# Seven half-size products in place of eight in the last batch's first channel product, with an order written out as a table and DMA issues on two queues

## The chip, the cores and the metric

The kernel runs on one core of a Trainium2 chip. The metric is the device time of one execution in microseconds (us), as the median of several runs. The core has five engines that run beside each other: TensorE (PE) multiplies matrices, VectorE (DVE), ScalarE (ACT) and GpSimd (POOL) work element by element, and SyncE (SP) issues DMAs. Each takes its instructions in the order of its own queue and waits on semaphores for the others.

## The reference

Four batches, 768 tokens, 8 heads of 64: window attention with four sink tokens, then one MLP block of a token product and two channel products.

```python
scores = where(keep, q @ k.T / sqrt(64), -1e9)      # keep: sink or within 128 tokens back
x = softmax(scores) @ v                             # (4, 768, 512)
tok = einsum('ts,bsd->btd', w_tok, alpha1 * x + beta1)
u = x + lam * tok
a2 = alpha2 * u + beta2
ch = maximum(a2 @ w_ch1, 0.0) @ w_ch2               # 512 -> 2048 -> 512
out = u + lam * ch
```

## The kernel before

Every piece of work is a *task*: a Python function that issues a few instructions, with a priority, the engines that may do it and the ns that each is thought to take, the tasks it comes after, and the buffers it uses. `plan.add` collects the tasks. At the end `plan.emit` sets the order. A planner (`Plan.run`) imitates the engines: it takes the task that can start soonest, breaks ties by priority, gives it an engine and a free buffer of its kind, and imitates the DMA rings as well (`Rings`). Priorities are shuffled a little by a list of thirty random seeds (`TURNS`) ahead of that. Where the planner sees TensorE idle in the first 36 us it adds short filler matmuls ("idle", L349) that keep its clock up.

Buffers come in kinds with a fixed number of places (`homes`). The ones that matter here: `d`, four PSUM banks for products; `S`, two pairs of PSUM banks for attention scores; `wst`, four buffers of SBUF for staged weights and, in batches 2 and 3, for the fp16 q and k of one head pair; `n16`, four; `nat`, eight, for loaded q and k, and later for sums; `vnat`, four, for loaded v; `x`, twelve rows of 128 tokens by 512; `uT` and `qkT`, one each; `hT`, two.

The stages of a batch, for the names in the profile:

- attention (`scores` L724, `pv` L825, and the normalising multiply L851): of batch b+1, spread among the products of batch b. In batches 2 and 3 q and k are loaded (L508), cast to fp16 and turned by a DMA transpose (L630); earlier by TensorE (`tp`).
- token product (`tok` L956): six row tiles of six matmuls. Then x gets the sum (L963), is cast (L356) into `u16`, transposed by DMA into `uT` (L1015) and scaled in place by alpha2 and beta2 (`affine`, L980 on ACT, L982 on DVE). Batch 0 transposes on TensorE (`uTp`).
- first channel product (`mlp1`, L1036): for each of two halves of the tokens (`chk`, 384 tokens) and each of 16 tiles of 128 hidden channels (`fi`) four matmuls that add over the 512 inputs into one `d` bank; then a relu into `hT` by ACT (L1042) or DVE (L1044).
- second channel product. Batch 0: `mlp2` (L1221). Batches 1 to 3: the 2 x 2 block product (token halves by channel halves) in Winograd's form with seven products P1 to P7 (`prod`, L1153) in place of eight. Its sums of weights (`w2_sums`, L1068) are made once, its sums of h (`h_sums`, L1094 to L1097, called S1 to S4) for every batch.

The weights of the first channel product are in `w1f` (128 x 4 x 2048, fp16), where the second index is the quarter of the 512 inputs. All DMAs but the casting loads (GpSimd) and five tiny ones at the start (ACT) are issued by SyncE.

Of the kernel before, what the change touches and what calls it, by code (L numbers as in the profile page):

```python
# [9 lines left out]
FP32 = mybir.dt.float32  # L10
# [7 lines left out]
SEEN = {PE: 200, ACT: 60, DVE: 60, POOL: 70}  # L18


class Buf:


    def __init__(self, kind, shape, dtype, name):
        self.kind, self.shape, self.dtype, self.name = kind, shape, dtype, name
        self.left = 0
        self.freed = 0.0
        self.home = None
        self.t = None


FW = 1.0

SWDONE = 1800.0


class Rings:


    WIRE = {"hw": 1600.0, "sw": 2100.0}  # L40

    HOLDS = 128.0

    def __init__(self):
        self.now = 0.0
        self.queue = {"hw": [], "sw": []}
        self.given = {"hw": [], "sw": []}

    def issue(self, ring, t, at):
        self.given[ring].append(t)  # L50
        self.queue[ring].append([t, float(t.lands[0]), float(t.lands[1]), at + self.WIRE[ring]])

    def room(self, ring, lands, at):

        keep = self.now, {r: [list(h) for h in q] for r, q in self.queue.items()}
        self.step(at)
        g = self.given[ring]
        last = g[-8] if len(g) >= 8 and g[-8].seen is None else None
        q = self.queue[ring]
        while last is not None and any(h[0] is last for h in q):  # L60
            self.step(float("inf"))
        over = sum(h[1] for h in q) + lands[0] - self.HOLDS
        while ring == "hw" and over > 0 and q:
            if q[0][1] < over:
                self.step(float("inf"))
                over = sum(h[1] for h in q) + lands[0] - self.HOLDS
            else:
                self.now += over * q[0][2]
                over = 0
        to = max(at, self.now)  # L70
        self.now, self.queue = keep
        return to

    def step(self, until):

        while True:
            heads = [(r, q[0]) for r, q in self.queue.items() if q]
            if not heads:
                return None
            live = [(r, h) for r, h in heads if h[3] <= self.now]  # L80
            later = [h[3] for r, h in heads if h[3] > self.now]
            turn = sum(h[2] for r, h in live)
            ends = [(self.now + h[1] * turn, r) for r, h in live]
            end = min(ends) if ends else (float("inf"), None)
            to = min([end[0], until] + later)
            for r, h in live:
                h[1] -= (to - self.now) / turn
            self.now = to
            if end[0] <= to:
                return self.queue[end[1]].pop(0)[0]  # L90
            if to >= until:
                return None

    def peek(self):

        keep = self.now, {r: [list(h) for h in q] for r, q in self.queue.items()}
        t = self.step(float("inf"))
        at = self.now if t else float("inf")
        self.now, self.queue = keep
        return at  # L100
# [11 lines left out]
class Plan:  # L112
# [19 lines left out]
    def run(self, prio):  # L132

        tasks = self.tasks
        rank = [0] * len(tasks)
        for r, i in enumerate(sorted(range(len(tasks)), key=lambda i: (prio[i], i))):
            rank[i] = r
        waiting = [len(t.needs) for t in tasks]
        ready = [t.since for t in tasks]
        homes = {k: [0.0] * n for k, n in self.homes.items()}  # L140
        busy = {k: [False] * n for k, n in self.homes.items()}
        for t in tasks:
            t.seen = None
            for b in t.uses:
                b.left, b.freed, b.home = 0, 0.0, None
        for t in tasks:
            for b in t.uses:
                b.left += 1
        free = {PE: 0.0, ACT: 3500.0, DVE: 3200.0, POOL: 500.0, SP: 0.0}
        rings = Rings()  # L150
        open_ = []
        steps = []

        def end(t, seen):
            t.seen = seen
            for b in t.uses:
                b.left -= 1
                b.freed = max(b.freed, seen)
                if b.left == 0:
                    busy[b.kind][b.home] = False  # L160
                    homes[b.kind][b.home] = b.freed
            for o in t.then:
                ready[o.i] = max(ready[o.i], seen)
                waiting[o.i] -= 1
                if not waiting[o.i]:
                    bisect.insort(open_, (rank[o.i], o.i))

        def pick():
            best = None
            spare = {k: sorted(h for h, x in zip(homes[k], busy[k]) if not x) for k in homes}  # L170
            for r, i in open_:
                at = ready[i]
                if best is not None and at > best[0]:
                    continue
                t = tasks[i]
                asked = {}
                for b in t.uses:
                    if b.home is None:
                        asked[b.kind] = asked.get(b.kind, 0) + 1
                if any(len(spare[k]) < n for k, n in asked.items()):  # L180
                    continue
                at = max([at] + [spare[k][n - 1] for k, n in asked.items()])
                own = None
                for e in t.engs:
                    at_e = max(free[e], at)
                    if e == POOL or (e == DVE and t.port):
                        at_e = max(at_e, port)
                    key = (at_e + FW * t.engs[e], at_e, r, at_e + t.engs[e], i, e)
                    if own is None or key < own:
                        own = key  # L190
                if best is None or own[1:] < best:
                    best = own[1:]
            return best

        open_ = sorted((rank[t.i], t.i) for t in tasks if not waiting[t.i])
        mode = None
        port = 0.0
        landing = float("inf")
        until, _, took = self.fill
        while len(steps) < len(tasks):  # L200
            best = pick()
            if best is None or landing <= best[0]:
                assert landing < float("inf"), "no task can go on"
                t = rings.step(float("inf"))
                end(t, rings.now + (SWDONE if POOL in t.engs else 300.0))
                landing = rings.peek()
                continue
            start, r, _, i, e = best
            open_.pop(bisect.bisect_left(open_, (r, i)))
            t = tasks[i]  # L210
            for b in t.uses:
                if b.home is None:
                    b.home = min((h, n) for n, (h, x) in enumerate(zip(homes[b.kind], busy[b.kind]))
                                 if not x)[1]
                    busy[b.kind][b.home] = True
            idle = None
            n = int((start - max(free[PE], 400.0)) / (took if free[PE] > 4500.0 else 110.0))
            if e == PE and free[PE] < until and n > 0:
                spare = [(h, k) for k, (h, x) in enumerate(zip(homes["d"], busy["d"])) if not x]
                if spare and min(spare)[0] <= free[PE]:  # L220
                    idle = (min(spare)[1], n)
                    homes["d"][idle[0]] = start
                    mode = None
            cost = t.engs[e]
            if t.lands:
                cost += rings.room("sw" if e == POOL else "hw", t.lands, start) - start
            if e == PE:
                if start < 4500.0:
                    cost = cost * 2
                if t.mode != mode:  # L230
                    cost = cost + 95
                mode = t.mode
            free[e] = start + cost
            if e == POOL or (e == DVE and t.port):
                port = free[e]
            steps.append((t, e, start, free[e], idle))
            if t.lands:
                rings.step(start)
                rings.issue("sw" if e == POOL else "hw", t, free[e])
                landing = rings.peek()  # L240
            else:
                end(t, free[e] + SEEN[e])
# [1187 lines left out]
```

The softmax here doesn't subtract the row's maximum and nothing guards it: scores larger than these inputs give would overflow.

## Time and profile before

| what | value |
|---|---|
| median of 3 runs | 256.87 us (256.66 to 257.07) |
| the profiled execution | 257.06 us, of it a span of 255.3 us from the first instruction to the last |
| granted TensorE clock | 0.999 |
| last token product of batch 3 ends | 212.84 us |
| first channel product of batch 3 | 212.84 to 233.63 us |
| second channel product of batch 3 | 233.63 to 252.01 us, then one add and the last store |
| one first-product matmul (L1036) | 128 x 384, 512 of them in all batches |
| relu of a product on ACT (L1042) | 0.49 us |
| relu of a product on DVE (L1044) | 0.55 us |
| add of a 256-column product on DVE (L1166) | 0.42 us |
| DMA transpose, from issue to landing | 2.4 us (`uT`), 2.8 us (`qkT`) |

The busy time of an engine is the time in which it works on an instruction; the chain of waits follows the end of the program back, at each step to what released it. Matmuls overlap, and their ends are modelled, so a long row of matmuls in the chain is TensorE without a gap.

### The profile page before, as it was taken

Reading aid. Unit: us, or ns where it says so; the run is one execution under the profiler, and the core shown is the slowest. Engines: PE = TensorE matmul, PEld = TensorE weight load, DVE = VectorE, ACT = ScalarE, POOL = GpSimd, SP = SyncE. Lnnn points to the kernel's source line nnn. Section 1 sums busy time; section 2 is a strip of 40 time slices with the busy share of each in tenths; the row PEclk is TensorE's granted clock in tenths of the full one; section 3 lists DMA queues with packets and bytes.
Section 4 is the critical chain, followed back from the end, with each engine's and each line's share of the span. In section 5 each row is a group of like instructions: output and inputs, shape, how many; then the busy total and the mean of one; then the engine's idle time right before and its main releaser. Section 6 shows DMA issues by size and latency. Waiting matters only on the chain.

```text
span 255.3 us, 5519 instructions
## 1 busy us (share of the span) xinstructions
PE 247.4 (97%) x2174; PEld 160.9 (63%) x2174; DVE 190.0 (74%) x402; ACT 142.6 (56%) x236; POOL 88.3 (35%) x108
## 2 busy tenths in 40 slices
PE   8999998999999999899999999999999999999994
PEld 7754645675555544456678676558668666667883
DVE  6777998696878878578889997877789764136782
ACT  2689845989848035688971225867571125775000
POOL 7409802344445330159653460735310101000000
PEclk9999999999999999999999999999999999999999
DMA  6998999999943998599778689501000156000105
GB/s 202 195 223 292 216 230 392 373 370 218 218 73 115 186 260 190 117 205 220 155 138 182 125 191 251 85 3 21 3 0 3 59 167 146 0 0 3 63 4 185
DMA packets 86130, 38.80 MB, mean 152 GB/s; under 512 B 73540, under 2 KB 80460, under 8 KB 86104
## 3 DMA queue, kind: packets, MB, share of 16 engines
q1 hardware_dynamic: 82320, 35.14, 56.5%
q0 software_dynamic: 3744, 3.28, 8.1%
q8 instruction: 17, 0.28, 0.5%
q14 instruction: 9, 0.07, 0.1%
q10 hardware_dynamic: 40, 0.03, 0.0%
HBM read 29.91 MB, written 6.29 MB: 142 GB/s over the span
## 4 chain that ended last, share of the span: by engine, by line
PE 88%; DMA 4%; DVE 3%; POOL 1%; issue 1%; ACT 1%; POOLq 0%; ACTq 0%
PE h L1036 33%; PE P L1153 21%; PE tok L956 11%; PE ch L1221 8%; PE pv L825 5%; PE S L724 4%; DMA n<-in_q_dram 4%; DVE uT L982 1%; PE S L719 1%; PE tp L614 1%; PE pv L818 1%; POOL n L497 1%; PE wT L916 1%; ACT uT L980 1%; DVE w2f L1068 1%
## 5 line engine op out<-in xcount | busy, mean ns | idle before, releaser
L1036 PE MATMUL h<-uT,w1f 128*128 128x384 f16 x512 | 91.9, 326 | 2.7 <-DVE uT L982 1.3
L1036 PEld LDWEIGHTS <-w1f 128*128 128x128 f16 x512 | 47.3, 98 | 34.5 <-issue 5.5
L1042 ACT ACTIVATE hT<-h 128x384 f16<-128x384 f32 x99 | 48.3, 492 | 26.1 <-PE h L1036 25.6
L1153 PEld LDWEIGHTS <-hT 128*128 128x128 f16 x408 | 39.8, 98 | 6.7
L746 ACT ACTIVATE E<-S 128x1024 f16<-128x1024 f32 (+1 forms) x39 | 37.9, 1001 | 7.5 <-PE S L724 3.7
L869 POOL TENSOR_TENSOR tm<-x,la_b 128x512 f32<-128x512 f32 x18 | 26.2, 1454 | 26.3 <-DVE xh L872 19.1
L956 PE MATMUL tok<-xh,wtokT 128*128 128x512 f16 x144 | 33.4, 379 | 0.0
L356 ACT CAST u<-x 128x512 f16<-128x512 f32 x19 | 11.7, 618 | 31.2 <-DVE x L963 31.1
L1153 PE MATMUL P<-w2f,hT 128*128 128x256 f16 x216 | 25.9, 273 | 0.0
L1166 DVE TENSOR_TENSOR x<-x,P 128x256 f32<-128x256 f32 x45 | 18.3, 418 | 8.2 <-PE P L1153 7.9
L1044 DVE TENSOR_SCALAR hT<-h 128x384 f16<-128x384 f32 x29 | 15.8, 553 | 10.9 <-PE h L1036 10.5
L956 PEld LDWEIGHTS <-wtokT 128*128 128x128 f16 x144 | 14.0, 98 | 14.6
L1221 PE MATMUL ch<-w2f,hT 128*128 128x512 f16 x96 | 23.0, 379 | 0.0
L1153 PE MATMUL P<-w2s,hT 128*128 128x256 f16 x192 | 22.8, 273 | 0.0
L851 DVE TENSOR_TENSOR x<-pv,rec 128x256 f32<-128x256 f32 x48 | 20.4, 424 | 1.7
L358 POOL CAST vfs<-vnat 128x512 f16<-128x512 f32 x18 | 15.0, 840 | 16.2 <-DMA vnat<-in_v_dram 16.0
L963 DVE TENSOR_TENSOR x<-x,tok 128x512 f32<-128x512 f32 x24 | 16.2, 684 | 5.7 <-PE tok L956 5.7
L356 ACT CAST n<-nat 128x768 f16<-128x768 f32 x16 | 13.2, 829 | 10.8 <-DMA nat<-in_q_dram 8.8
L825 PEld LDWEIGHTS <-E 128*128 128x128 f16 x328 | 15.2, 97 | 6.0 <-issue 1.6
L825 PE MATMUL pv<-vfs,E 128*128 128x65 f16 x328 | 17.9, 194 | 0.0
L358 POOL CAST u<-x 128x512 f16<-128x512 f32 x5 | 3.1, 621 | 34.8 <-DVE x L963 21.1
L1221 PEld LDWEIGHTS <-hT 128*128 128x128 f16 x96 | 8.6, 98 | 9.1 <-issue 0.2
(131 smaller groups left out, 327.4 us busy)
## 6 DMA issues: line engine op xcount, KB each, us to landing
out_dram<-x SPq DMA_DIRECT2D x21, 256.0 KB, 2.8
nat<-in_q_dram SPq DMA_DIRECT2D x13, 384.0 KB, 5.3
nat<-in_k_dram SPq DMA_DIRECT2D x13, 384.0 KB, 5.7
vnat<-in_v_dram SPq DMA_DIRECT2D x18, 256.0 KB, 5.2
wst_w<-in_moe_w_ch_dram SPq DMA_DIRECT2D x8, 512.0 KB, 7.4
wtn<-in_moe_w_tok_dram SPq DMA_DIRECT2D x6, 384.0 KB, 4.7
w1f<-in_moe_w_ch_dram POOLq DMA_DIRECT2D x4, 512.0 KB, 11.1
v<-in_v_dram SPq DMA_DIRECT2D x12, 128.0 KB, 6.4
```

The source lines that it names most:

```text
L356: nc.scalar.copy(o, i)
L358: engine[e].tensor_copy(o, i)
L746: nc.scalar.activation(eT.t, pS.t[:, :, 0 : n * w].rearrange("p e (i w) -> p e i w", i=n), AF.Exp, scale=scale)
L825: nc.tensor.matmul(po.t[:, hl, :], eT.t[:, e_, off + i, c : c + P], vf[j][:, h, :], start=(r < 2 and n == 0), stop=(n == len(parts) - 1 an ...
L851: nc.vector.tensor_mul(bx.t[:, 4 * G : 4 * G + 4, :], po.t[:, :, 0:D], rec.t.to_broadcast([P, 4, D]))
L869: engine[e].tensor_mul(bt.t, bx.t.rearrange("p h d -> p (h d)"), la1_b)
L956: nc.tensor.matmul(pt.t, wtokT[:, si, ti * P : (ti + 1) * P], hs[si].t, start=(si == 0), stop=(si == NR - 1))
L1036: nc.tensor.matmul(ph.t, w1f[:, c, fi * P : (fi + 1) * P], bu.t[:, c, chk * NTOK : (chk + 1) * NTOK], start=(c == 0), stop=(c == NC - 1))
L1042: nc.scalar.activation(bh.t[:, fi, :], ph.t, AF.Relu)
L1153: nc.tensor.matmul(pc.t, hh[:, nt * P : (nt + 1) * P], w(fi), start=(first and n_ == 0), stop=(n_ == HF - 1), skip_group_check=True)
L1166: nc.vector.tensor_add(row(bx)[:, cols], row(bx)[:, cols], pc.t)
L1221: nc.tensor.matmul(pc.t, bh.t[:, fi, nt * P : (nt + 1) * P], w2f[:, fi, :], start=(fi == 0), stop=(fi == NF - 1))
```

## The change

Three things change together.

**The first channel product of batch 3.** It takes Winograd's form too. The blocks are: token halves c0 and c1 of `uT`, input halves (quarters 0-1 and 2-3), and hidden tiles i and i + 8. For each pair of tiles (i, i + 8), i = 0 to 7, seven products P1 to P7 of two matmuls stand where four tiles of four matmuls stood. `NPL = 0` says that no pair keeps the plain form.

```diff
+    HSUM = 3
+    NPL = 0
+    def w1_sums(p):
+        n = (HF - NPL) * P
+        for w in ("S1", "S2", "S4"):
+            w1s[w] = Buf("wst", [P, 2, n], FP16, f"w1{w}")
...
+            sub(0, "S1", lambda g, c: g.tensor_add(b1.t[:, c], w1f[:, c, k_], w1f[:, 2 + c, k_]), [done["w1", 3]], [b1])
+            sub(1, "S2", lambda g, c: g.tensor_sub(b2.t[:, c], b1.t[:, c], w1f[:, c, f]), [done["w1S1", c]], [b1, b2])
+            sub(2, "S4", lambda g, c: g.tensor_sub(b4.t[:, c], w1f[:, 2 + c, f], b2.t[:, c]), [done["w1S2", c]], [b2, b4])
+            sub(3, "S3", lambda g, c: g.tensor_sub(w1f[:, c, k_], w1f[:, c, f], w1f[:, c, k_]),
+                [done["w1S1", c]] + late, [])
...
+    def u_sums(p, b):
+        for w in ("T1", "T2", "T3", "T4"):
+            uS[w] = Buf("n16", [P, 2, NTOK], FP16, f"u{w}")
...
+        sub(0, "T3", lambda g: g.tensor_sub(t3.t, bu.t[:, 2:4, c1], bu.t[:, 0:2, c1]), ud(0, 0) + ud(1, 0) + ud(1, 1), [t3])
+        sub(0.1, "T1", lambda g: g.tensor_sub(t1.t, bu.t[:, 0:2, c1], bu.t[:, 0:2, c0]), ud(0, 0) + ud(1, 0), [t1])
+        sub(0.2, "T2", lambda g: g.tensor_sub(t2.t, bu.t[:, 2:4, c1], t1.t), [done["uT1"]] + ud(1, 1), [t1, t2])
+        sub(0.3, "T4", lambda g: g.tensor_sub(t4.t, bu.t[:, 2:4, c0], t2.t), [done["uT2"]] + ud(0, 1), [t2, t4])
```

`mlp1_pair` takes one `S` buffer (two banks, V and Q), one `d` bank X for P2, two fp32 buffers of kind `vnat` and one of kind `x`. P1 goes to V and is read out; P6 adds to V and is read out; P5 adds to V and is read out; P3 adds to V, and its relu is one tile of h. P2 goes to X, and adding P1's copy gives the second tile. P7 goes to Q; the sum with P5's copy gives the third. P4 adds to Q; with P6's copy it gives the fourth. These three sums are an add on DVE (fp32 copy + PSUM, into `hT`) and a relu in place on ACT, DVE or POOL.

```diff
+        def mm(e):
+            for c in range(2):
+                nc.tensor.matmul(acc(), lhs(c), rhs(c), start=first and c == 0, stop=c == 1, skip_group_check=True)
+        before = {"P6": "P1", "P5": "P6", "P3": "P5", "P4": "P7"}.get(what)
+        if before:
+            after = after + [done["hread", before, i]]
...
+        def plus(bx, chk, fi, more, acc=acc):
+            bh = hT[b, chk]
+            r = add(p + 0.05, {DVE: 485}, lambda e: nc.vector.tensor_add(bh.t[:, fi, :], bx.t, acc()), [a] + more, [po, bx, bh])
...
+        if what == "P1":
+            done["hread", "P1", i] = read(ba)
+        elif what == "P2":
+            plus(ba, 0, i, [done["hread", "P1", i]])
+        elif what == "P6":
+            done["hread", "P6", i] = read(bb)
+        elif what == "P5":
+            done["hread", "P5", i] = r = read(bc)
+            done["hread", "P7", i] = plus(bc, 1, HF + i, [r, done["hp", "P7", i]], lambda: two.t[:, 1, 0:NTOK])
+        elif what == "P4":
+            plus(bb, 0, HF + i, [done["hread", "P6", i]])
```

**The order.** The planner, its ring model and the seeds go. In their place are four tables: `ORDER`, the numbers of all 1227 tasks in the order in which they are issued; `ENGINES`, a digit for each task; `HOMES`, a place for each buffer; `IDLES`, where filler matmuls stand. The costs at `plan.add` and the spacing of priorities (`PAR`) change too, but the tables alone set what is issued. The order differs from the one before in all batches.

```diff
-    def emit(self, turns):
-        prio = [t.prio for t in self.tasks]
-        for seed in turns:
-            prio = shuffle(prio, seed)
-        for t, e, start, stop, idle in self.run(prio):
+    def emit(self, order, engines, homes, idles):
+        own = iter(homes)
+        for t in self.tasks:
             for b in t.uses:
                 if b.home is None:
+                    b.home = int(next(own), 16)
+        fills = {i: (home, n) for i, home, n in idles}
+        for i in order:
+            t = self.tasks[i]
+            e = (ACT, DVE, PE, POOL, SP)[int(engines[i])]
+            idle = fills.get(i)
...
+    IDLES = (
+        (46, 0, 64), (53, 0, 2), (90, 1, 6), (107, 1, 13), (111, 1, 3), (150, 2, 1), (158, 0, 1),
+    )
```

**Two queues.** Plain loads and stores may be issued by SyncE or by ACT; transposes stay with SyncE.

```diff
+    queue = {SP: nc.sync, ACT: nc.scalar}
...
-                p, {SP: 480}, lambda e: nc.sync.dma_start(bf.t, src), [wait], [bf], lands=(16, {(0, 0, 1): 85, (0, 1, 0): 140}.get((b, hp, t), 72)))
+                p, {SP: 480, ACT: 550}, lambda e: queue[e].dma_start(bf.t, src), [wait], [bf], lands=(16, {(0, 0, 1): 85, (0, 1, 0): 140}.get((b, hp, t), 68)))
```

By the tables 27 issues are ACT's: one load of w_tok, ten of q and k, six of v, and ten stores, two in batch 0 and eight in the later ones.

## The prediction

> **What bounds the kernel now.** I read the page's shares first, then the chain of waits, then what TensorE waited for, then groups and windows of the last batch.
>
> ```profile
> PE 247.4 (97%) x2174; PEld 160.9 (63%) x2174; DVE 190.0 (74%) x402; ACT 142.6 (56%) x236; POOL 88.3 (35%) x108
> ...
> DVE  6777998696878878578889997877789764136782
> ACT  2689845989848035688971225867571125775000
> ```
>
> TensorE fills 97% of the span, so only two things can shorten it: fewer matmuls, or fewer TensorE gaps. In the slices, DVE and ACT thin out in the last fifth, where no next batch's attention is left.
>
> The chain of waits (start us, us, what) ends in one unbroken run of matmuls:
>
> ```profile
> 211.54 1.29 PE tok L956 x6
> 212.84 20.80 PE h L1036 x128
> 233.63 18.35 PE P L1153 x168
> 252.01 0.42 DVE x L1166
> ```
>
> 20.80 us is the first channel product of the last batch: 128 matmuls of 384 columns, 162.5 ns each, no gap. The 18.35 us behind it (second product) and the last add and store are no part of the edit. TensorE's waits, longest in total (us, times, longest):
>
> ```profile
> PE h L1036 <- DVE uT L982: 1.3, 2, 1.1
> ...
> PE h L1036 <- ACT uT L980: 0.9, 2, 0.5
> ...
> PE h L1036 <- DVE x L1166: 0.4, 1, 0.4
> ```
>
> They lie at 39.8-41.4 us (start of batch 0's first product, 0.47 + 0.19 + 0.38), 101.8-103.4 (batch 1's, 1.07 and a little) and 180.2. The same stretches in the timeline:
>
> ```profile
> 39.78 0.32 PE L1036 MATMUL h<-uT,w1f 128*128 128x384 f16 x1 [0.47 <-ACT uT L980]
> ...
> 102.83 2.49 PE L1036 MATMUL h<-uT,w1f 128*128 128x384 f16 x12 [1.07 <-DVE uT L982]
> ```
>
> Windows of the last two stages, and of the time from 19 us to them, show what room the evacuating engines have:
>
> ```profile
> 212.70:233.50 20.80, 20.80 (x130) 12.52 (x129) 5.77 (x9) 15.18 (x31) 0.61 (x1) 1.00 0.11 27
> 233.50:252.05 18.55, 18.47 (x169) 16.31 (x167) 14.24 (x30) 0.88 (x3) 0.00 (x0) 1.00 0.20 72
> 19.00:212.70 193.70, 190.97 (x1643) 119.11 (x1640) 156.22 (x323) 115.65 (x186) 79.37 (x85) 1.00 0.72 169
> ```
>
> After the length: PE, PEld, DVE, ACT, POOL busy. In the first product DVE has 15.0 us free, ACT 5.6. From 19 to 212.7 us TensorE idles 2.7 us.
>
> **What the Trainium skill says.** "TensorE: Matmul & The Clock Gate", section "Wait — 56ns, not 53.3ns?": a warm matmul costs its columns over 2.4 GHz and about 2.5 ns; for 384 columns 162.5 ns, and the trace agrees to the digit (20.80 / 128). The same page, "Architectural detail": ACT and DVE are strict first-in-first-out, so an instruction that waits holds all behind it. "DMA: Bandwidth & Descriptors", section "Issuing engines are not separate DMA queues": issuing from several engines saves only the time of the issue; no run here shows it. "SBUF — State Buffer", section "Who interferes with whom": a DVE operation with two SBUF inputs contends with a GpSimd operation that reads SBUF; the trace of before has such adds (0.42 us for 512 fp16 columns, one of 0.55), too few to settle it.
>
> **The change, part by part.** The sum is made against the profiled execution: 257.06 us, of it a span of 255.3. The median shown is 256.87, 0.19 lower. The written-out order is numbers, but counting the tasks in the order in which the code adds them gives each number its name, and so each engine's order and each tile's buffer.
>
> *Products.* Each of 8 tile pairs has 7 products of 2 matmuls where it had 4 x 4: 112 for 128, all of 384 columns. 16 x 162.5 ns = 2.6 us less.
>
> *Waits inside the pairs.* A pair's bank is now read three times between products (P1, P6, P5, P3 share one bank, P7 and P4 the other). A product that needs a read can start after: 0.16 us drain and 0.04 to ACT (h ends 233.63 by the model, ACT starts 233.67), the read 0.49 (L1042), 0.04 back: 0.73 us from the last issue of the one to the first of the other. A product issues in 0.33. Two pairs run interleaved, so two other products (0.65) usually stand between: 0.08 short, about twice a round. Where the next two pairs take over the banks, the last relu and add (0.49 on ACT, 0.55 on DVE, between 0.42 for 256 and 0.68 for 512 columns) are in the way. Laying out the queues of all three engines in the new order with these durations, I get for the four rounds waits of 0.1, 0.3 + 0.15, 0.15 + 0.15 and 0.5, and 0.1 in the last round: 1.4 us in all. The ends: 0.6 if reads overlap better (ACT instructions back to back start closer than their duration), 4 if DVE lags. For DVE is nearly full: 23 adds at 0.48 (spacing when back to back), three sums of u at 0.47, three of h at 0.88 (of eight; four lay in this stage before), some nine relus, two reads and two adds of batch 2 come to 18.8 us in a stage of 19.8.
>
> *Entry.* All pairs need sums of both halves of u. After the last token product seven products of batch 2 and five of the pairs (7 x 0.873 + 5 x 0.33 = 7.75 us) are queued; the add (0.69), cast (0.62), transpose (2.4), affines and two sums come to about 7.5 us by DVE's queue, seven adds included. Hidden by 0.2 us; each further us late costs one.
>
> *Sums of w1.* Eight of 1024 fp16 columns, by the mask multiply of the same size (0.73) 5.8 us, seven on DVE and one on POOL in batches 0 to 2; the last two overwrite w1 beside batch 2's second product. They take three of the four staging buffers "wst" for good. Batch 3's q and k therefore go through one buffer, a head pair after the other. The last pair's load waits for batch 2's sum buffer (product P7 of batch 1); from there 0.5 us issue, 5.3 landing (median), two casts 1.6, two transposes 2.5 and 2.8 give 12.7 us, and 15.4 us of matmuls stand before its first score. Hidden, with 2.7 us to spare.
>
> *Moves.* Batch 0's h now starts behind a whole token product (1.29 us) that covers the affines: 0.9 of its 1.04 us goes. In batch 1 the first three token products come first, and 7.0 us of other matmuls follow before h, against about 6.6 us for add, cast, transposes and affines: 0.9 of 1.17 goes, and the next thing late would be the last affine on DVE, behind three adds. At 180 us h waited for a PSUM buffer that two adds had to read; the new order gives it another: 0.3 of 0.37. Together 2.1 (ends: 0 and 2.4).
>
> *Start.* q and k of the first heads are asked for before the 384 KB of w_tok that now lead SyncE's queue. The filler matmuls behind the first transpose are 26 for 43. But all loads share 16 engines that are 90% busy from 6 us on, and POOL now has a multiply ahead of its last load (1.45 us in L869 for that size). I take 0.5 us of gain; ends 1.5 and a loss of 1.
>
> *Two queues.* 27 issues go to ACT's queue. In the trace ACT's own issues took 0.27 to 0.58 us: some 14 us of ACT, spread over 250, and each with a wait holds what is behind it. Some stand before exps and relus in batches 0 and 1. With the DVE sums above and small new gaps of any reorder I put this at 1.0 us lost; ends 0 (ACT idles 113 us) and 5.
>
> Sum: -2.6 + 1.4 - 2.1 - 0.5 + 1.0 = -2.8; 257.06 - 2.8 = 254.3, and on the scale of the median **254.1 us**.
>
> **The rivals.**
> *All of it.* Waits in pairs 0.6, gaps 2.4, start 1.0, nothing lost: -5.4, 251.5 us. For it: ACT and DVE are free in that stage. Against: TensorE's order is in-line, and four dependent reads a pair don't vanish.
> *DVE paces the pairs.* If an add costs its whole 0.55 and a relu its whole latency, DVE's 18.8 becomes 21.5, the stage is longer than the 20.8 of now, and the saved matmuls are given back: +0.7 for -1.2, total -0.9, 256.0 us. For it: 95% full with waits in line. Against: adds back to back start 0.33 us apart where one lasts 0.42.
> *ACT's queue holds TensorE* (the slower side). The stores and loads that SyncE now takes sat there waiting for as much as 26 us at no cost; on ACT an issue that waits for a buffer or a DVE add holds exps and relus, and scores and h stop when their two or four PSUM buffers are full. If one in three of the 27 holds TensorE for its 0.54 us, 4.9 us are lost in place of 1.0: 258.0; with half of the closed gaps lost to it too, 259.0. It decides from 3.8 us lost, 0.14 us an issue. Against: most are placed behind their waits.
> That the products are not saved isn't a rival: the loop has no plain h left for the last batch.
>
> **How the numbers follow.** Forecast 0.55, all of it 0.13, DVE paces 0.15, ACT's queue 0.17. About 0.2%, 0.5 us, is what a measurement can tell from no change. The forecast's own ends are 252 to 256.5; the first rival asks for 251.5 and below, part of the last for 258 and over. 8 in 10: 251.2 to 258.2. Faster: nearly all of the first two, half of the third: 0.68. Same 0.08, slower 0.24, the last rival and half of the reach of the third.
>
> **What would show it.** Right: 112 matmuls in the pairs with TensorE waits of 1 to 2 us among them, each for an ACT read or DVE add; no wait of over 0.3 us at the start of batches 0's and 1's h; the second product of batch 3 still about 18.4 us. Wrong: a DVE busy without a gap through the pairs while TensorE waits over 3 us; scores of batch 3 waiting for transposes; ACT issues just ahead of TensorE gaps in batches 0 to 2; first transposes later than now (7.5 us).

## The result and the profile after

| | before | after |
|---|---|---|
| median | 256.97 us (256.66 to 258.39, 4 runs) | 267.96 us (266.63 to 269.61, 4 runs) |
| the profiled execution | 257.06 us, span 255.3 | 266.63 us, span 264.9 |
| granted TensorE clock | 0.999 | 0.991 |

The ratio is 1.042, with a 95% interval of 1.034 to 1.050: slower. The page of the changed kernel, shares and slices:

```profile
PE 247.2 (93%) x2142; PEld 159.0 (60%) x2142; DVE 209.3 (79%) x449; ACT 138.5 (52%) x230; POOL 113.9 (43%) x130
...
DVE  6495899789989863898999895867589896778981
ACT  1559853888984141899532235766613446663000
```

TensorE is busy for as long as before (247.2 us for 247.4), though it has 32 matmuls less (16 of the products and 16 fillers); its idle time grew from 7.9 to 17.7 us. DVE took 19 us more, and the thin last fifth of its row has filled up. The two traces side by side say where the 9.6 us of span went. Batch 2's last products stand among the pairs now, and some of batch 3's second product; the table takes them out at 0.109 us for a matmul (32 of them ahead of the stage, which starts at 212.33 us, and 8 behind it, which ends at 241.48 us). The start of batch 0's product before is taken without its waits: 41.38 us less three matmuls that had run by then.

| up to | before | after | late by |
|---|---|---|---|
| batch 0's first product runs | 40.89 | 43.94 | 3.05 |
| start of batch 3's first product | 212.84 | 215.82 | 2.98 |
| end of batch 3's first product | 233.63 | 240.61 | 6.98 |
| the last add ends | 252.43 | 259.40 | 6.97 |
| the span ends | 255.3 | 264.9 | 9.6 |

Three places, then: 3.0 us ahead of batch 0's product, 4.0 us in the pairs, where the sum had 1.2 us less, and 2.6 us behind the last add. What TensorE waited for (us in all, times, longest; `hp` are the two banks V and Q of a pair):

```profile
PE hp L1028 <- DVE hT L1042: 2.5, 5, 0.5
PE h L935 <- DVE uT L881: 2.1, 1, 2.1
PE pv L724 <- ACT E L645: 1.9, 1, 1.9
PE tok L855 <- DVE x L862: 1.1, 1, 1.1
...
PE hp L1028 <- ACT hT L1069: 0.6, 2, 0.5
PE hp L1028 <- ACT hb L155: 0.4, 2, 0.2
```

**The start.** The timeline of ACT and of TensorE at 16 to 21 us:

```profile
16.14 0.61 ACT L645 ACTIVATE E<-S 128x512 f16<-128x512 f32 x1
19.70 0.35 ACTq L441 DMA_DIRECT2D wtn<-in_moe_w_tok_dram  x1
20.10 1.02 ACT L645 ACTIVATE E<-S 128x1024 f16<-128x1024 f32 x1 [3.35 <-DMA v<-in_v_dram]
...
21.18 0.43 PE L724 MATMUL pv<-vfs,E 128*128 128x65 f16 x7 [1.86 <-ACT E L645]
```

ACT does nothing from 16.75 to 19.70 us: the next thing in its queue is the issue of a load of w_tok, and what ends its idle time is the landing of a load of v, which has no buffer in common with it. The chain of waits names that load:

```profile
14.98 4.70 DMA v<-in_v_dram
19.70 0.35 ACTq L441
```

In the trace the issues of SyncE and ACT take eight completion semaphores in turn (numbers 107, 109, 111 and 113 to 117). The issue at 19.70 us takes number 109, which the load of v at 14.98 us had taken eight issues before, and so it waits for that load to land. The exp behind it is 3.35 us late, and TensorE waits 1.86 us for that exp. From 20 to 25 us the granted clock is 0.66. One more 1.05 us goes at 41.4 us: two adds of DVE (L780) take 2.81 us beside two products of GpSimd (L837, 2.94 us); the same add takes 0.65 us at 37.2. The Trainium skill, "SBUF — State Buffer", section "Who interferes with whom", says that a DVE operation with two SBUF inputs contends with a GpSimd operation that reads SBUF; these numbers agree.

**The pairs.** The chain of waits through the first round (start, us, what):

```profile
218.42 0.74 PE hp L1028 x4
219.16 0.02 issue
219.19 0.49 ACT hc L155
219.68 0.02 issue
219.70 0.56 DVE hT L1042
220.26 0.04 issue
220.31 0.82 PE hp L1028 x4
221.13 0.02 issue
221.16 0.50 ACT hT L1069
...
222.15 0.56 DVE hT L1042
222.71 0.02 issue
222.73 0.50 ACT hT L1069
```

TensorE, ACT and DVE take turns. At 219.19 ACT reads bank V into `hc` and is done at 219.67; then DVE's add at 219.70 reads bank **Q**; only behind that does TensorE go on at 220.31, with P3, which writes bank **V**. ACT had been done with V 0.6 us before. In the same way a relu of ACT, which reads V (L1069), stands behind adds of DVE that read Q, though both only read. A pair's V and Q are one buffer of two banks (`hp`), and the waits are made by buffer.

**The end.** The last stores in the timeline, and the last add:

```profile
256.27 4.62 SPq L1192 DMA_DIRECT2D out_dram<-x  x4
...
257.05 3.86 ACTq L1192 DMA_DIRECT2D out_dram<-x  x5
...
258.98 0.42 DVE L1186 TENSOR_TENSOR x<-x,P 128x256 f32<-128x256 f32 x1 [0.45 <-PE P L1173]
```

All nine stores of batch 3's second product are issued from 256.3 us on. Before, they began at 236.7. Three of them follow P2 and its add, and their data is complete more than 15 us before the end; in the order they stand near its end, two on ACT's queue and one on SyncE's, behind stores of later products. From the last add to the end it takes 5.5 us in this execution; before it took 2.9.

### The profile page after: what moved, and what is told of

Same layout as the page of the kernel before. It is cut to its first block, busy times and chain, and to the rows that moved or that the text cites. A ratio compares the mean times of both kernels' runs of the same rounds, so it can differ in the third digit from the quotient of the medians.

```text
span 264.9 us, 5543 instructions
## 1 busy us (share of the span) xinstructions
PE 247.2 (93%) x2142; PEld 159.0 (60%) x2142; DVE 209.3 (79%) x449; ACT 138.5 (52%) x230; POOL 113.9 (43%) x130
## 4 chain that ended last, share of the span: by engine, by line
PE 79%; DMA 5%; DVE 5%; SPq 4%; ACT 3%; issue 2%; ACTq 0%; DVEq 0%
PE h L935 24%; PE P L1173 21%; PE tok L855 8%; PE ch L1241 7%; PE pv L724 5%; PE hp L1028 5%; DMA v<-in_v_dram 4%; PE S L623 3%; DVE hT L1042 2%; SPq L441 1%; DVE x L780 1%; PE S L618 1%; PE pv L717 1%; SPq L430 1%; DMA uT<-u 1%
## 5 line engine op out<-in xcount | busy, mean ns | idle before, releaser
L935 PE MATMUL h<-uT,w1f 128*128 128x384 f16 x384 | 68.7, 326 | 2.1 <-DVE uT L881 2.1
L935 PEld LDWEIGHTS <-w1f 128*128 128x128 f16 x384 | 35.6, 98 | 24.8 <-issue 4.4
L1173 PEld LDWEIGHTS <-hT 128*128 128x128 f16 x408 | 39.8, 98 | 7.1 <-issue 0.2
L768 POOL TENSOR_TENSOR tm<-x,la_b 128x512 f32<-128x512 f32 x18 | 24.6, 1368 | 37.6 <-DVE rec L749 15.1
L943 DVE TENSOR_SCALAR hT<-h 128x384 f16<-128x384 f32 x47 | 25.4, 553 | 7.8 <-PE h L935 7.1
L941 ACT ACTIVATE hT<-h 128x384 f16<-128x384 f32 x49 | 23.3, 492 | 13.4 <-PE h L935 13.1
L155 ACT CAST n<-nat 128x768 f16<-128x768 f32 x21 | 17.1, 832 | 16.3 <-DMA qkT<-n 12.8
L724 PE MATMUL pv<-vfs,E 128*128 128x65 f16 x328 | 18.2, 196 | 1.9 <-ACT E L645 1.9
L585 POOL TENSOR_SCALAR_AFFINE_SELECT E<-E 128x512 f16<-128x512 f16 x20 | 13.1, 681 | 14.4 <-ACT E L645 14.3
L157 POOL CAST vfs<-vnat 128x512 f16<-128x512 f32 x18 | 12.2, 692 | 12.2 <-DMA vnat<-in_v_dram 5.9
L749 DVE RECIPROCAL rec<-pv 128x4 f32<-128x4 f32 x48 | 8.5, 177 | 8.7 <-PE pv L724 8.1
```

The source lines that it names most:

```text
L155: nc.scalar.copy(o, i)
L724: nc.tensor.matmul(po.t[:, hl, :], eT.t[:, e_, off + i, c : c + P], vf[j][:, h, :], start=(r < 2 and n == 0), stop=(n == len(parts) - 1 an ...
L768: engine[e].tensor_mul(bt.t, bx.t.rearrange("p h d -> p (h d)"), la1_b)
L935: nc.tensor.matmul(ph.t, w1f[:, c, fi * P : (fi + 1) * P], bu.t[:, c, chk * NTOK : (chk + 1) * NTOK], start=(c == 0), stop=(c == NC - 1))
L941: nc.scalar.activation(bh.t[:, fi, :], ph.t, AF.Relu)
L943: nc.vector.tensor_scalar_max(bh.t[:, fi, :], ph.t, 0.0)
```

## The experiments

Each kernel below has 4 to 22 runs. They come in four sets: all issues on SyncE, V and Q as two buffers, early stores and the three together; one issue alone, the re-ordered hand-over and the fillers; late stores, the re-ordered version again and plain pairs; plain pairs again, without and with the sums. Each set ran on one chip, beside the kernel before, whose median was 256.79 to 256.93 us there, for 256.97 beside the changed kernel; a comparison across sets is uncertain by about that difference.

### All DMA issues on SyncE

The digit of 27 tasks in `ENGINES` becomes SyncE's; the order stays.

```diff
-        "2020201202010202020202020213213213213213213202002020202020213121312131213121312131044444"
+        "2020201202010202020202020213213213213213213202002020202020213121312131213121312131444444"
...
```

> The changed kernel with one thing other: the 27 DMA issues that stand on ScalarE's queue (loads and stores) are issued by SyncE, at the same places of the written-out order. Theory A (ScalarE's queue holds TensorE at the start: its issue of the third w_tok load waits for a landing, and exps stand behind it): TensorE's wait of 1.86 us for the exp near 21 us goes, the dip of the granted clock at 20 to 25 us goes with it, batch 0's first h product starts 2 to 3 us earlier than 43.9 us, and the time falls from 268 to about 265. Theory B (the loads and SyncE's single queue set the start, whoever issues them): less than 1 us of difference, or slower, since the issue's wait now holds SyncE's transposes. The pair stage (24.9 us) stays in both; the tail stays at 5.5 us or grows by the issues that SyncE now does one after the other.

Measured: 264.15 us (263.98 to 266.71), 3.8 less than the changed kernel. The wait of pv is gone, batch 0's product starts at 41.11 us in place of 43.94, and the time is the one of theory A. The clock dip, which theory A had expected to go too, moved to 10 to 15 us (0.66), behind a wait of 0.90 us for a load of q. The tail of this execution is 4.5 us for 5.5. That 1.0 us isn't shown to come from the edit: with the end of the program unchanged, the profiled executions of two kernels below (one issue alone, two buffers) have a tail of 3.9 us.

### One of them alone

```diff
# the task of the load of w_tok's fourth block
-ENGINES: ACT
+ENGINES: SP
```

> The changed kernel with one thing other: of its 27 issues on ScalarE's queue only one, the load of the fourth block of w_tok, goes to SyncE, at its place in the order. Theory A (that one issue, which waits for the landing of an earlier DMA with an exp behind it, makes the whole loss at the start): the wait of 1.9 us of the pv product near 21 us goes, batch 0's first h product starts at about 41 us in place of 43.9, as with all 27 moved (41.1), and the time is 264.5 to 265.5. Theory B (several of the issues on ScalarE share the loss): the start lies between, at 42 to 43.5 us, and the time above 266.

Measured: 265.55 us (265.10 to 268.95), 2.4 of the 3.8 us; four of six runs at 265.1 to 265.9. The median lies at the upper end of theory A's 264.5 to 265.5, but no trace shows where batch 0's product starts in such a run: the profiled execution is the slowest of the six, and it shows the next issue that waits. The timeline of its ACT:

```profile
35.93 0.62 ACT L155 CAST u<-x 128x512 f16<-128x512 f32 x1 [1.69 <-DVE x L862]
40.15 0.41 ACTq L403 DMA_DIRECT2D nat<-in_q_dram  x1
40.60 0.62 ACT L155 CAST u<-x 128x512 f16<-128x512 f32 x1 [4.05 <-DMA wst_w<-in_moe_w_ch_dram]
```

The issue of a load of q waited for the landing of a load of w_ch, the cast of u behind it came 4.05 us later, and TensorE waited 3.07 us for that. Whichever issue happens to meet a late landing holds ACT. In this sense theory B, that several issues share the loss, is right too.

### V and Q as two buffers

```diff
-        "S": (ps, [P, 2, 512], FP32),
+        "S": (sps, [P, 2, 512], FP32),     # closed at the first pair
...
-            return px.t if into == "X" else two.t[:, "VQ".index(into), 0:NTOK]
+            return px.t if into == "X" else two.t["VQ".index(into)][:, 0:NTOK]
...
+        return [pair_ps[0].tile([P, 512], FP32, tag=f"{x}_{b.home}", bufs=1, name=f"{b.name}{x}") for x in "vq"]
```

> The changed kernel with one thing other: a pair's two PSUM banks (V, in which P3, P6, P5 and P1 add up, and Q, for P7 and P4) are two buffers of one bank each in place of one buffer of two; order, engines and operations are the same. Theory A (waits are set by buffer and not by bank, so that a product into V waits for a read of Q and the other way round): the pair stage falls from 24.9 us to 20 to 21 us, TensorE's waits for DVE's and ScalarE's reads of hp fall from about 6.7 us to 1 to 2.5 us, and the time falls by about 4 us, from 268 to 264. Theory B (VectorE paces the pairs: its adds, sums and relus fill the stage): VectorE is already over 90% busy there, the stage stays at 24 us or more and the time within 1 us of 268.

Measured: 262.42 us (260.84 to 263.79), 5.5 less. The same stretch of the program in windows, length first, then PE, PEld, DVE, ACT, POOL busy. The changed kernel:

```profile
212.33:241.48 29.15, 25.17 (x154) 14.78 (x153) 22.10 (x49) 17.11 (x38) 7.17 (x5) 1.00 0.17 60
```

and with two buffers:

```profile
212.86:237.01 24.15, 23.77 (x154) 14.73 (x153) 22.27 (x50) 16.81 (x39) 7.17 (x5) 1.00 0.21 72
```

DVE and ACT do the same work, to 0.3 us; the stretch is 5.0 us shorter. It holds 112 matmuls of 384 columns (18.2 us) and, by the order, 40 of 256 (4.37 us), 22.57 us in all: 6.6 us of waits before, 1.6 after. In the list of waits `hp` has one entry left (0.2 us, for ACT). DVE is busy for 92% of the stretch and yet holds TensorE up little, so theory B falls. As nothing but the buffers changed, the cause is shown: the waits go by buffer. The Trainium skill, "PSUM — Partial Sum Buffer", section "Summary: rules for kernel authors", says to guard reads of PSUM by bank; here that is worth 5 us.

### The early stores where their data is ready

```diff
# ORDER, ENGINES: the three stores that follow P2's adds
-near the end of the order, two on ACT and one on SP
+directly behind these adds, all three on SP
```

> The changed kernel with one thing other: the three stores of the last batch's first column half of the token half c0 (those that follow product P2 and its add, complete some 15 us before the end) stand directly behind their adds in the order, on SyncE, and not at the very end of ScalarE's queue. Theory A (nine last stores meet at the end because early ones stand behind late ones): from the last add to the end of the span 3 to 4 us in place of 5.5, the time 1.5 to 2.5 us lower, about 266. Theory B (a last store takes that long whatever stands before it): less than 0.5 us.

Measured: 267.48 us (264.51 to 270.21), no difference that the median could settle. In the profiled execution, the slowest of the six, the last add ends at 264.67 us and the span at 267.6: 2.9 us, as before the change, for 5.5. The tail is as short as theory A says, but that execution waited 3.3 us at the start for ACT's exp, and the scatter of the start hides what the tail gains. The price is measured again below.

### The three together

> The three edits of the other kernels of this set together: all DMA issues on SyncE, a pair's two banks as two buffers, the three early stores at the place where their data is ready. If the three costs are separate stretches of TensorE's path (start, pairs, tail), the gains add: 2.5 + 4 + 2 = 8.5 us, 259 to 260, still above the kernel before by what the start of batch 1's h and VectorE's load cost. If one limit (VectorE, or SyncE's queue) stands behind them, the sum of the three singles is not reached, and the time stays above 262.

Measured: 257.47 us (255.77 to 260.45), 10.5 less; ratio to the kernel before 1.0019 (0.9995 to 1.0043). The single gains add up to 9.8 (0.5 of it, of the stores, within the scatter), so they are separate stretches and no common limit stood behind them; the 8.5 that had been expected were too low. A wait that remains is at batch 1's product, where TensorE waits 2.5 us (2.1 in the changed kernel). There the chain of waits of the changed kernel reads:

```profile
98.38 0.70 DVE x L862
...
99.10 0.63 ACT u L155
99.73 1.19 SPq L529
...
101.02 1.22 SPq L914
...
102.33 1.22 SPq L914
...
103.64 2.82 DMA uT<-u
...
106.58 0.97 DVE uT L881 x3
```

9.2 us from the add to the product: a transpose of q and k (L529) is issued ahead of those of u (L914), and each holds SyncE's queue for 1.2 us.

### Batch 1's hand-over re-ordered

```diff
# ORDER on SyncE: transposes of u for batch 1's first half ahead of
+uT 1, uT 2, uT 0
 store of batch 0, last transpose of q and k of batch 2, load of v
-uT 1, uT 2, uT 0
# the cast of u's row tile 2: GpSimd
+# ScalarE
# TensorE: first scores of batch 2
+# behind the second h tile of batch 1
```

> The version with all three edits, and the hand-over to batch 1's first product re-ordered: the three transposes of u for its first half go on SyncE's queue ahead of the last transpose of q and k, one store and one load of v; the second of these three casts of u is made by ScalarE and not by GpSimd; the first scores of batch 2 stand behind two h tiles and not ahead of them. Theory A (the transposes of u stand in SyncE's queue behind work that nobody waits for yet, and one cast behind GpSimd's casts of v): batch 1's first h product loses its wait of 2.5 us, and the time falls by 2 to 2.5 us from 257.5 to about 255.2. Theory B (VectorE's adds or the transposes themselves, 1.2 us each on one ring, set it): a wait of 1.5 us or more stays and the time falls by less than 1 us.

Measured: 255.24 us (253.62 to 257.26), ratio 0.9934 (0.9912 to 0.9956). This is theory A, to 0.1 us. SyncE's timeline there, first with the three edits alone:

```profile
97.71 1.26 SPq L533 DMA_TRANSPOSE qkT<-n  x1
99.08 0.52 SPq L417 DMA_DIRECT2D vnat<-in_v_dram  x1
99.65 3.90 SPq L918 DMA_TRANSPOSE uT<-u  x3
```

and re-ordered:

```profile
96.59 3.83 SPq L918 DMA_TRANSPOSE uT<-u  x3
100.47 0.57 SPq L1259 DMA_DIRECT2D out_dram<-x  x1
101.10 1.26 SPq L533 DMA_TRANSPOSE qkT<-n  x1
```

The third transpose of u lands at 101.6 us, for 104.8 without the re-ordering, and the wait of 2.5 us shrinks to 0.2. How much of this each of the three parts of the edit brings isn't separated. A second measurement of the same kernel, below, gave 255.81.

### Filler matmuls at the start

```diff
-        (46, 0, 64), (53, 0, 2), (90, 1, 6), (107, 1, 13), (111, 1, 3), (150, 2, 1), (158, 0, 1),
+        (46, 0, 64), (53, 0, 2), (90, 1, 6), (51, 1, 14), (61, 1, 6), (107, 1, 13), (111, 1, 3), (150, 2, 1), (158, 0, 1),
```

> The re-ordered version and 20 more filler matmuls at the start: 14 ahead of the transposes of q that wait for their load at 10 us, 6 ahead of the last ones near 18 us. The runs of the version with all three edits fall in two groups by the granted clock: 255.8 to 257.6 us at 0.995 and above, 258.1 to 260.5 at 0.993 and below. Theory A (TensorE's idle time of about 1 us near 10 us takes its clock to a lower step in some runs, and the filler matmuls that the change removed kept it up): with the fillers nearly all runs show a clock of 0.995 or more, the scatter shrinks to about 1 us and the median falls by 1 to 1.5 us against the same kernel without them. Theory B (the clock is lost elsewhere, or the fillers delay the transposes): the scatter stays, and the median is the same or higher by up to 0.5 us.

Measured: 256.39 us (254.78 to 258.63) for 255.24 without, 1.15 slower. The first half of theory A holds: all 22 runs show a clock of 0.997 or more, while the second set of the kernel without fillers, below, has 8 of 22 runs under 0.995 (median 256.97 us, for 255.60 of the other 14). The second half, a faster kernel, doesn't: the dips were rare in that set without fillers too (0.993 in one of 18 runs, 0.995 and above in the others), so little was to be had back; the 20 matmuls take TensorE 1.1 us (20 of 0.056), and six of them waited 0.57 us for their own bank. That is the delay of theory B, larger than it said. The runs still scatter over 3.9 us at full clock, so the clock isn't all of the scatter; what else it is stays open.

### Stores late again, on SyncE

```diff
# ORDER of the re-ordered version: the three early stores back at the end, still on SP
```

> The re-ordered version with the three early stores of the last batch back at their late places in the order, but on SyncE. Theory A (a store that is placed late in the order is paid at the end, on any queue): the stretch from the last add to the end grows from 3.4 us by 0.7 to 2 us, and the time with it, to about 256 to 257 us. Theory B (it was ScalarE's queue that delayed them): no change within 0.5 us.

> The re-ordered version once more, as the thing that the other two kernels of this set are compared with on the same chip: 255.2 us by the first run, with a scatter of 253.6 to 257.3.

Measured: 257.59 us (256.03 to 259.15) with late stores, 255.81 us (253.29 to 258.62) without. From the last add to the end it takes 4.5 us for 3.1. This is theory A: the place in the order costs it, on SyncE as well. With late stores SyncE's timeline has

```profile
249.67 4.84 SPq L1196 DMA_DIRECT2D out_dram<-x  x9
```

and without

```profile
235.81 15.18 SPq L1196 DMA_DIRECT2D out_dram<-x  x9
```

The late one's median may contain some of the start's scatter; its tail, 1.4 us longer, doesn't. Over all profiled executions the tail is 3.9 to 5.5 us with these stores late (5.5, 3.9 and 3.9 on two queues, 4.5 and 4.5 on SyncE) and 2.9 to 3.4 us with early stores or in the kernel before: the 2.6 us of the changed kernel's profile are the upper end of what the place costs.

### The pairs in the plain form

```diff
-            for c in range(2):
-                nc.tensor.matmul(acc(), lhs(c), rhs(c), start=first and c == 0, stop=c == 1, skip_group_check=True)
+            if h0 is not None:      # P2, P1, P7, P3; P4, P5, P6 issue nothing
+                for c in range(4):
+                    nc.tensor.matmul(acc(), w1f[:, c, h0 * P:(h0 + 1) * P], bu.t[:, c, chk * NTOK:(chk + 1) * NTOK], start=c == 0, stop=c == 3)
...
-                    p + 4 * c + q, {DVE: 75 + n * 0.52, POOL: 300 + n * 2.1}, lambda e: made(engine[e], c), after, uses, port=True)
+                    p + 4 * c + q, {DVE: 75 + n * 0.52, POOL: 300 + n * 2.1}, lambda e: None, after, uses, port=True)
```

> The re-ordered version with the pairs of batch 3 computed in the plain form: each of 8 pairs is four tiles of four matmuls again, at the places of P2, P1, P7 and P3, relu straight from PSUM, two bank buffers; the sums of w1 and of u and the adds and reads within the pairs are left out. Everything else, order and queues too, stays. Theory A (seven products for eight are worth what the sum said, 2.6 us of matmuls less 1.3 to 1.6 us of waits, and the sums are hidden): 1 to 1.5 us slower than the re-ordered version, 256.3 to 256.8 us. Theory B (the sums of w1 and the adds on VectorE cost as much elsewhere as the products bring): within 0.5 us of 255.2 us, or faster.

> The version with plain pairs and no sums once more, as the thing that the kernel with the sums is compared with on the same chip: 254.6 us by the first run; if that was luck, as much as the 255.2 to 255.8 us of the re-ordered version with seven products.

Measured: 254.61 us (254.44 to 254.96) and, in a second set, 254.59 us (253.84 to 254.94); ratios to the kernel before 0.9916 (0.9903 to 0.9929) and 0.9903 (0.9882 to 0.9925). The re-ordered version with seven products had 255.24 and 255.81. So, over the whole kernel, seven products with their sums are no faster than eight: theory B. In the stage itself the seven do save. The same stretch with seven, in the re-ordered version:

```profile
208.78:232.70 23.92, 23.77 (x155) 14.74 (x153) 22.15 (x50) 16.86 (x39) 7.18 (x5) 1.00 0.21 72
```

and with eight, in the second set:

```profile
206.24:231.74 25.50, 25.50 (x170) 16.45 (x169) 15.34 (x31) 7.69 (x16) 0.00 (x0) 1.00 0.20 68
```

It is 1.58 us less with seven. That is lost ahead of the stage, where the kernel with seven is 2.54 us behind (208.78 for 206.24 us). The last kernel shows the larger part of it.

### Plain pairs, with the sums

```diff
-                    lambda e: None, after, uses, port=True)
+                    (lambda e: made(engine[e], c)) if name != "S3" else (lambda e: None), after, uses, port=True)
...
-            done["u" + name] = add(p + q, {DVE: 475, POOL: 1750}, lambda e: None, after, [bu] + uses, port=True)
+            done["u" + name] = add(p + q, {DVE: 475, POOL: 1750}, lambda e: made(engine[e]), after, [bu] + uses, port=True)
```

> The version with plain pairs, and with six of the eight sums of w1 and all four sums of u put back at their places (their results are used by nobody; the two sums that overwrite w1 stay left out). Theory A (the sums, on VectorE and GpSimd beside batches 0 to 2 and the entry of the pairs, open the TensorE gaps in which the saving of the seven products is lost): TensorE's idle time from 42 to 205 us grows from 0 to about 1 us, and the time from 254.6 to 255.5 us or more. Theory B (the sums are hidden, and the plain version is faster for its luck at the start): no idle time from 42 to 205 us, and a time within 0.3 us of the plain version without sums, measured beside it.

Measured: 255.73 us (254.43 to 257.59) with the sums, 254.59 without. This is theory A. Batch 0's product starts at the same time in both profiled executions (39.76 and 39.74 us). Then, in a window of the one with sums:

```profile
42.00:104.00 62.00, 60.96 (x474) 33.57 (x471) 51.95 (x102) 39.12 (x61) 30.85 (x30) 1.00 1.00 218
```

and without:

```profile
42.00:104.00 62.00, 62.00 (x482) 34.23 (x480) 47.65 (x99) 40.19 (x63) 27.27 (x30) 1.00 1.04 229
```

DVE has 4.3 us more to do from 42 to 104 us, and TensorE, which was without a gap, idles 1.04 us there, in two waits of 0.5 us for DVE. At batch 2's last long row of products (205.19 us for 203.62) the kernel with the sums is 1.57 us behind. The re-ordered version with seven products (second set) idles 0.94 us there:

```profile
42.00:104.00 62.00, 61.06 (x470) 33.73 (x469) 49.78 (x102) 39.99 (x62) 32.42 (x33) 1.00 1.03 230
```

So the sums give back most of what the product form brings. They don't explain all of the 2.54 us: 1.1 us of it stands already at batch 0's product, which starts at 40.84 us with seven products (40.58 in the first set) and at 39.7 in both plain kernels and in the one with the sums. What makes that part stays open.

## Why the prediction was wrong

It said 254.1 us with a range of 251.2 to 258.2; the time is 267.96. Against the profiled execution the sum had -2.8 and 9.6 was measured. Of the 12.4 us between, 5.2 are in the pairs, about 4.5 at the start and 2.6 behind the last add. From batch 0's product to the pairs the sum had -0.2 (with the 1.0 us for queues and small gaps) and the table has -0.1, but by luck, as the moves show. By its steps:

- *Products*: right. 16 matmuls less, 2.6 us at 162.5 ns each; they are there again in the version with plain pairs.
- *Waits inside the pairs*: the step that failed most. The sum had 1.4 us, with 4 as its end; 6.6 were measured. The durations in it were right, and with V and Q as two buffers the waits are 1.35 to 1.6 us. What it took for granted is that P3 waits only for reads of V and P4 only for reads of Q. The code declares one two-bank buffer for both, and the runs show that each product waited for the reads of either. That could have been read in the code: `pair` makes one `Buf("S", ...)` for two banks.
- *Entry*: right, no wait ahead of the first round; batch 3's scores didn't wait either.
- *Sums of w1*: hidden behind TensorE they were not. Their place was read correctly, but their cost stood only within the 1.0 us of small gaps. Measured, ten of the twelve sums of w1 and u together: 1.1 us by the medians, 1.57 in the traces.
- *Moves*: -0.9 at batch 0, -0.9 at batch 1, -0.3 at 180 us. The wait at 180 us is gone, and so are those at batch 0's product, but a new one of 1.05 us stands ahead of it, at the token product. At batch 1 the wait grew from 1.07 to 2.13, because the chain is 9.2 us long and not 6.6: I had counted one transpose of 2.4 us, not the three that SyncE issues 1.2 us apart, with one of q and k ahead. Re-ordering the hand-over gained 2.2 us.
- *Start*: -0.5 with ends of -1.5 and +1. With batch 0's -0.9, the prediction had the first product 1.4 us earlier; it came 3.05 later. ACT's queue makes most of it: moving all its issues brought the start forward by 2.8 us, and moving one took 2.4 us off the time.
- *Two queues*: the mechanism was the third rival's, that an issue with a wait holds the exps behind it, but its place was the start and its price another: not 0.54 us an issue for one in three, but 1.9 to 3.3 us for one that waits for a landing. Its "most are placed behind their waits" overlooked a wait that no buffer explains. The Trainium skill, "DMA: Bandwidth & Descriptors", section "Issuing engines are not separate DMA queues", has it that a second issuing engine saves only the issue; nothing here contradicts this, and the kernels with one issuing engine were the faster.
- *The second product, the last add and the store* were called no part of the edit. The products weren't (17.48 us and 0.87 for 18.35). The stores were: the order is written out for them as well. The term of nothing for them measured 2.6 us in the profiled execution, and 0.5 to 2.6 over all traces with late stores against those with early ones.

Of the rivals, "DVE paces the pairs" is out: with two buffers DVE has 22.3 us of work in the stretch, more than the 18.8 of the sum, and still leaves TensorE only 1.6 us of waits. "ACT's queue holds TensorE" had the sign and about a third of the loss. *All of it*, 251.5 us, was not reached in any run of any kernel (the lowest is 253.29). The three edits together take away 10.5 of the 11.0 us.

The fastest version found computes plain pairs and keeps only the mended order: 254.6 us, 0.8 to 1.0% under the kernel before. The change's products bring 1.58 us in their stage, and its sums cost 1.1 to 1.57 us elsewhere; a later start of 0.8 to 1.1 us with seven products stays unexplained.

## What to carry to other kernels

Before pricing waits around PSUM, write down which buffer each read and write belongs to: if two banks are one buffer, a product waits for the reads of both, and dependent steps that should overlap become a chain of 0.5 us turns. A DMA issue on an engine that computes is priced by the longest landing that it can wait for, not by its own 0.4 us. When a change replaces the whole order, follow the last stores and every shared queue too, for nothing in it is untouched; and where sums buy matmuls, price them at the place where the summing engine is fullest.

## What the runs showed of the hardware

- TensorE's clock fell to half after gaps of one or two microseconds, for 3.4 us in each of these two traces. Windows that end and begin where it falls (length, then PE, PEld, DVE, ACT, POOL busy; the 1.00 or 0.50 behind them is the granted clock), first of the changed kernel, then with all issues on SyncE:

```profile
17.96:21.37 3.41, 1.55 (x25) 0.88 (x21) 1.76 (x4) 1.27 (x2) 2.79 (x4) 1.00 0.98 231
21.37:24.79 3.42, 3.42 (x32) 1.60 (x29) 1.95 (x7) 3.36 (x8) 2.24 (x3) 0.50 0.97 307
...
7.53:10.94 3.41, 2.16 (x34) 1.29 (x33) 1.20 (x3) 2.36 (x4) 2.67 (x5) 1.00 1.21 216
10.94:14.35 3.41, 3.41 (x32) 2.12 (x29) 1.83 (x3) 0.87 (x3) 0.88 (x2) 0.50 1.29 216
```

  In the 3.41 us ahead of the fall TensorE idled 1.86 us in the one and 1.25 us in the other, of it 0.90 in one wait. At half clock 13 filler matmuls took 1.57 us, for 0.90 at full. With the three edits together a wait of 1.18 us at the same place was not followed by a fall. The Trainium skill, "TensorE: Matmul & The Clock Gate", section "What's actually happening", puts the fall after an idle window of about 3.4 us that runs freely; the length agrees, but the 3.41 us ahead of these falls were idle for only 55 and 37% of it. How much idle time is enough isn't shown.
- DMA transposes leave SyncE one each 1.2 us (1.22 and 1.22 us in the chain, three in 3.83 us), while one lands 2.4 to 2.8 us after its issue. Three in a row take 5.4 us in that chain, from the first issue at 101.02 us to the last landing at 106.46 us.
